# Seven products from the sixth chunk on, their weight sums formed earlier and brought by GpSimd's queue

## The chip, the cores and the metric

The kernel runs on one core of a Trainium2 chip. The metric is the device time of one execution in microseconds, median of several runs. The kernel before takes 916.63 us (three runs, 916.19 to 918.40).

## The reference, cut to what matters

Attention with pooled keys and values, and behind it a two-layer feed-forward network on the attention's output, all in fp32:

```
q, k, v: 8 batches x 8 heads x 576 x 64;   w_in: 512 x 2048;   w_out: 2048 x 512
k_p, v_p = mean of k, v over 8 neighbours       # 576 -> 72 keys
attn = softmax(q k_p^T / 8) ; o = attn v_p       # 8 x 8 x 576 x 64
x = o, heads side by side                        # 4608 tokens x 512
h = x @ w_in ; g = max(0.01 h, h) ; out = g @ w_out
```

## The kernel before, in words

The 4608 tokens are cut into nine chunks of 512 tokens, c0 to c8. The hidden 2048 columns are cut into 16 blocks of 128, f0 to f15, two of which form a "pair" later. TensorE has no fp32 product of full precision in this form, so each fp32 operand is held as a high part and the remainder (tiles xh and xl, gh and gl, pT_hi and pT_lo), and a product is three matmuls: high by high, low by high, high by low.

**Plain chunks.** For each f, the first layer takes 12 matmuls of 128x512 into one PSUM bank (`m1`, L1143 to L1145). ScalarE applies the leaky ReLU in place (L1148) and casts the high part gh (L1151), VectorE subtracts for gl (L1152). Two f's later the second layer takes 12 matmuls (`add_up`, L1354 to L1356) into four accumulators, one for each 128 tokens. At a chunk's end these are copied out and stored (`store`). So TensorE does 24 matmuls of 512 columns for one f, 48 for two.

**Seven-product chunks.** From chunk FAST on (before: c6, c7, c8), the first layer of a pair is one product of 2x2 blocks, done with seven products of half-size blocks instead of eight. Each is 6 matmuls of 128x256 (`product`, L1261), 42 for a pair, and the second layer's 24 matmuls follow (`pair`). The sums of blocks of x (T1 to T4) are made by `combine` (GpSimd L798, ScalarE L793, VectorE L794). The sums of blocks of w_in (S1 to S4, and the block A22 for the first four pairs) do not depend on x. They are formed once for each of the eight pairs, in the plain chunks, by `prepare`: nine VectorE additions of 128x256 (L1183), four ScalarE casts (L1186) and four VectorE subtractions (L1190), with the tile x_tail as scratch. High and low parts are put in "places", the unused second halves of the next chunk's x tiles, and from there stored to a DRAM tensor `kept` with eight transfers of 128 KB (L1217), and one of 256 KB for A22 (L1220). When the pair is multiplied, `stream` (L1253) brings the sums back, three loads for a pair: S1 with S2 (512 KB) into one "seat", S3 (256 KB) into a half of a w tile, S4 with A22 (512 or 256 KB) into another seat. The first pair's loads are issued by SyncE, the others by ScalarE's queue, each as soon as the product that reads the old contents is done; nothing is loaded for a chunk's last pair, since the next chunk runs the pairs in reverse.

**Attention beside it.** The attention of the next chunk's tokens runs in small steps ("units") that are dealt out between the matmuls of a chunk: scores (pss, L600), maximum (L608), exponential (L610), normalising on GpSimd (L644, L650; tile `at`), then a transposition through DRAM: SyncE stores rows (L661) and fetches blocks (L670), VectorE transposes them (L681, tile pp), ScalarE and VectorE split them (L703, L706, L710), and TensorE multiplies with v (pa, L725 to L728). The sums over 8 keys or values are made by GpSimd (L265, L272) from tiles that SyncE loads (L288, L305, L318).

**What sets the order.** TensorE's order is written out by hand throughout. In the plain chunks c0 to c5 the other engines' instructions are put in an order by the framework's scheduler from that. From the first seven-product chunk on GpSimd and SyncE are taken in the order of the program as well. `PLAN` says in which run of a chunk the weight sums are formed: (how many pairs, from which beat, until which). The runs are: c0 and c1 with f0 to f7 (run 0; runs 1 and 2, a half of c1 each), c1 with f8 to f15 (run 3), c0 with f8 to f15 (run 4, named REST), and then c2 to c8 whole.

Of the kernel before, what the change touches and what calls it, by code (L numbers as in the profile page):

```python
# [10 lines left out]
F32 = mybir.dt.float32  # L11
# [13 lines left out]
def tile_pooled_attention_ffn(  # L25
# [9 lines left out]
    nc = tc.nc  # L35
# [34 lines left out]
    VIA = 2  # L70
    SPLIT = 8
    HALF = CH // 2
    FAST = 6
    NEAR = (FAST + 1) % 2


# [1047 lines left out]
    REST = len(runs) - 1  # L1124
# [47 lines left out]
    def prepare(j, places):  # L1172

        f0, f1 = PAIRS[j]
        (a11, a12), (a21, a22) = (
            [[ws[0, f].bitcast(F32)[:, part, half] for part in range(2)]
             for half in (slice(0, HALF), slice(HALF, DM))] for f in (f0, f1)
        )
        u, w = (x_tail[:, 2 * i : 2 * i + 2, :].rearrange("p k x -> p (k x)") for i in range(2))
        ADD, SUB = ALU.add, ALU.subtract  # L1180

        def do(out, a, b, op):
            nc.vector.tensor_tensor(out, a, b, op=op)  # L1183

        def high(i, of):
            nc.scalar.copy(places[i][0], of)  # L1186

        def low(i, of):
            h, l = places[i]
            nc.vector.tensor_tensor(l, of, h.bitcast(F32), op=SUB)  # L1190

        do(u, a21[0], a21[1], ADD)
        do(w, u, a22[0], ADD)
        yield
        do(w, w, a22[1], ADD)
        high(1, w)
        do(u, a11[0], u, SUB)
        yield
        do(u, u, a11[1], ADD)
        high(0, u)  # L1200
        low(1, w)
        yield
        do(w, w, a11[0], SUB)
        low(0, u)
        yield
        do(w, w, a11[1], SUB)
        high(2, w)
        do(u, a12[0], w, SUB)
        yield
        do(u, u, a12[1], ADD)  # L1210
        high(3, u)
        low(2, w)
        yield
        low(3, u)
        for i, parts_of in enumerate(places):
            for k, part in enumerate(parts_of):
                nc.sync.dma_start(kept[j, :, i, k, :], part.bitcast(F32))  # L1217
        if j < OPEN:
            with tc.issue_after(sent[-1].ins):
                nc.sync.dma_start(kept[j, :, 4], ws[0, f1].bitcast(F32)[:, :, HALF:])  # L1220
        yield

    def free(n, i):

        if n < REST + FAST - 2:
            return [(h[:, HALF:], l[:, HALF:]) for h, l in zip(*x_parts(runs[n][0] + 1))]
        side, part = (runs[n][0] + 2) % 2, "hl"[i % 2]
        x = [one.tile([P, CH], F32R, tag=f"x{part}{side}_{kk}", name=f"place{i}_{kk}") for kk in range(NK)]
        return [(y[:, :HALF], y[:, HALF:]) for y in x]
# [36 lines left out]
    def pair(n, c, j, then, old, hooks):  # L1266


        f0, f1 = PAIRS[j]
        x = sums[c]  # L1270
        a11, a12 = ws[0, f0][:, :, :HALF], ws[0, f0][:, :, HALF:]
        a22 = seat("A22") if j < OPEN else ws[0, f1][:, :, HALF:]
        nm = f"{n}_{j}"
        pa, pc = ends_x[:, :HALF], ends_x[:, HALF:]
        pd, pe = ends_y[:, :HALF], ends_y[:, HALF:]
        off = one.tile([P, CH], F32, tag=f"xh{1 - NEAR}_{NK - 1}", name=f"off{nm}")
        dia = one.tile([P, CH], F32, tag=f"xl{1 - NEAR}_{NK - 1}", name=f"dia{nm}")

        def after(k):
            if hooks:  # L1280
                hooks[k]()

        def some(m):
            for _ in range(min(m, len(old))):
                old.pop(0)()
                yield

        def halves(w):
            h = three.tile([P, CH], F32R, tag="gh", name=f"gh{nm}")
            l = three.tile([P, CH], F32R, tag="gl", name=f"gl{nm}")  # L1290
            nc.scalar.copy(h, w)
            nc.vector.tensor_tensor(l, w, h.bitcast(F32), op=ALU.subtract)
            return h, l

        def load(name, ins):
            if then is not None:
                with tc.issue_after(ins.ins):
                    stream(nc.scalar, then, name)

        product(pa, a11, x["B11"], True)  # L1300
        product(pc, seat("S1"), x["T1"], False)
        with tc.high_priority():
            nc.scalar.copy(pd, pa)
            nc.scalar.copy(dia[:, HALF:], pc)
        yield
        yield from some(3)

        product(pd, seat("S2"), x["T2"], False)
        product(pa, a12, x["B21"], False)
        with tc.high_priority():  # L1310
            nc.vector.tensor_tensor(pe, pd, dia[:, HALF:], op=ALU.add)
            load("S1", nc.scalar.activation(dia[:, :HALF], pa, AF.Prelu, alpha=0.01))
        after(0)
        yield
        yield from some(2)

        product(pd, seat("S3"), x["T3"], False)
        with tc.high_priority():
            nc.vector.tensor_tensor(dia[:, HALF:], pd, dia[:, HALF:], op=ALU.add)
            load("S3", nc.scalar.activation(dia[:, HALF:], dia[:, HALF:], AF.Prelu, alpha=0.01))  # L1320
            gd = halves(dia)
        after(1)
        yield
        yield from some(len(old))

        product(pe, seat("S4"), x["B22"], False)
        product(pd, a22, x["T4"], False)
        with tc.high_priority():
            load("S4", nc.scalar.activation(off, ends_y, AF.Prelu, alpha=0.01))
            go = halves(off)  # L1330
        after(2)
        yield

        for f, t, g, i in (
            (f0, 0, gd, 0), (f0, 1, gd, 1), (f1, 2, gd, 2), (f1, 3, gd, 3),
            (f1, 0, go, 0), (f1, 1, go, 1), (f0, 2, go, 2), (f0, 3, go, 3),
        ):
            old.append(lambda f=f, t=t, g=g, i=i: second(n, c, f, t, g, i))
# [142 lines left out]
    for n, pieces in enumerate(beside):  # L1481
        us = [att[b][u] for b, u in line_up([x for x in pieces if x[0] < VIA])]
        us += [
            att[x[0]][x[1]] if x else lambda: None
            for x in line_of(n, [x for x in pieces if x[0] >= VIA])
        ]
        if n == 0:

            cut = us.index(att[1]["au01"]) + 1
            us, rest = us[:cut], us[cut:]  # L1490

            us.remove(att[1]["sa20"])
            us.insert(us.index(att[1]["au00"]) + 1, att[1]["sa20"])
            us = [att[0][u] for u in TAIL_STEPS.split()] + us
        elif n == 1:
            us = rest
        if n == REST:

            units[-1] = [lambda: None] * AHEAD + us[:AHEAD]
            us = us[AHEAD:]  # L1500
        units.append(us)
# [8 lines left out]
    for b, n in loads_at.items():  # L1510
        early[max(n, REST) - 1].append(b)

    PLAN = {REST + 1: (2, 10, 36), REST + 2: (3, 3, 34), REST + 3: (1, 3, 20), REST + 4: (2, 3, 34)}
    STEPS_OF = 7
    left = list(range(len(PAIRS)))

# [5 lines left out]
    for n, (c, fs, ts) in enumerate(runs[: REST + FAST - 1]):  # L1522
        us = list(units[n])
# [137 lines left out]
```

## Time and profile before

| | |
|---|---|
| median of the runs | 916.63 us (916.19 to 918.40) |
| the profiled execution | 919.39 us; span from first to last instruction 917.6 us |
| mean granted TensorE clock | 0.991 |
| busy: TensorE, VectorE, ScalarE, GpSimd | 886.1, 515.8, 447.4, 223.6 us |
| stages in the span | c0 and c1 until 212 us; run 4 212 to 264; c2 264 to 361; c3 361 to 457; c4 457 to 553; c5 553 to 640; c6 640 to 736; c7 736 to 824; c8 from 824 |

The stages are told apart by the program's names in the timeline of TensorE. The span is 1.8 us shorter than the time of the same execution. A row of the timeline gives the start of an instruction and its length; matmuls overlap, so the pace is read from one start to the next, not from the length.

### The profile page before, as it was taken

Reading aid. Unit: us, or ns where it says so; the run is one execution under the profiler, and the core shown is the slowest. Engines: PE = TensorE matmul, PEld = TensorE weight load, DVE = VectorE, ACT = ScalarE, POOL = GpSimd, SP = SyncE. Lnnn points to the kernel's source line nnn. Section 1 sums busy time; section 2 is a strip of 40 time slices with the busy share of each in tenths; the row PEclk is TensorE's granted clock in tenths of the full one; section 3 lists DMA queues with packets and bytes.
Section 4 is the critical chain, followed back from the end, with each engine's and each line's share of the span. In section 5 each row is a group of like instructions: output and inputs, shape, how many; then the busy total and the mean of one; then the engine's idle time right before and its main releaser. Section 6 shows DMA issues by size and latency. Waiting matters only on the chain.

```text
span 917.6 us, 14146 instructions
## 1 busy us (share of the span) xinstructions
PE 886.1 (97%) x4731; PEld 764.1 (83%) x4731; DVE 515.8 (56%) x1229; ACT 447.4 (49%) x1397; POOL 223.6 (24%) x394
## 2 busy tenths in 40 slices
PE   5599999999999999999999999999999999999998
PEld 4478888788887888888888888888999999999997
DVE  6999569546276654774465537655665653342222
ACT  5788559345344534443454336354654553453322
POOL 4511110352534231412133132514320230010000
PEclk9889999999999999999999999999999999999999
DMA  9965231327357342834245317630785255425332
GB/s 266 313 203 171 64 76 47 88 61 197 102 163 169 109 96 53 230 93 109 53 141 118 97 36 195 162 102 3 198 212 148 67 148 144 122 78 161 104 113 72
DMA packets 157464, 116.53 MB, mean 127 GB/s; under 512 B 100688, under 2 KB 136016, under 8 KB 157392
## 3 DMA queue, kind: packets, MB, share of 16 engines
q1 hardware_dynamic: 145488, 90.86, 36.7%
q10 hardware_dynamic: 11904, 24.78, 9.4%
q8 instruction: 37, 0.61, 0.3%
q14 instruction: 35, 0.29, 0.1%
HBM read 85.07 MB, written 30.54 MB: 126 GB/s over the span
## 4 chain that ended last, share of the span: by engine, by line
PE 84%; DVE 7%; ACT 3%; DMA 2%; POOL 1%; issue 1%; SPq 1%; POOLq 0%; DVEq 0%; ACTq 0%
PE acc L1354 13%; PE acc L1355 13%; PE acc L1356 13%; PE ph L1143 8%; PE ph L1144 8%; PE ph L1145 8%; PE ends_y L1261 7%; PE ends_x L1261 6%; PE pss L600 3%; DMA kremraw<-in_k_dram 1%; PE pa L726 1%; DMA blocks<-rows 1%; PE pa L728 1%; PE pa L727 1%; PE pa L725 1%
## 5 line engine op out<-in xcount | busy, mean ns | idle before, releaser
L1354 PE MATMUL acc<-w,gh 128*128 128x512 f32 x576 | 228.2, 396 | 0.7 <-DVE o L1394 0.7
L1355 PE MATMUL acc<-w,gh 128*128 128x512 f32 x576 | 225.9, 392 | 0.0
L1356 PE MATMUL acc<-w,gl 128*128 128x512 f32 x576 | 225.0, 391 | 0.0
L1143 PE MATMUL ph<-xh,w 128*128 128x512 f32 (+1 forms) x416 | 159.5, 384 | 0.6 <-DVE gl L1152 0.6
L1144 PE MATMUL ph<-xl,w 128*128 128x512 f32 (+1 forms) x416 | 156.5, 376 | 0.0
L1145 PE MATMUL ph<-xh,w 128*128 128x512 f32 (+1 forms) x416 | 156.3, 376 | 0.0
L1356 PEld LDWEIGHTS acc<-w,gl 128*128 128x128 f32 x576 | 108.4, 188 | 23.5
L1354 PEld LDWEIGHTS acc<-w,gh 128*128 128x128 f32 x576 | 108.7, 189 | 20.1 <-issue 1.1
L1355 PEld LDWEIGHTS acc<-w,gh 128*128 128x128 f32 x576 | 108.7, 189 | 18.1
L610 ACT ACTIVATE e<-pss,red 128x72 f32<-128x72 f32 (+1 forms) x320 | 97.8, 329 | 44.6 <-DVE red L608 44.5
L1148 ACT ACTIVATE ph<-ph 128x512 f32<-128x512 f32 (+1 forms) x104 | 57.7, 555 | 94.8 <-PE ph L1145 94.3
L1152 DVE TENSOR_TENSOR gl<-ph,gh 128x512 fp32r<-128x512 f32 (+1 forms) x104 | 66.8, 642 | 61.3 <-ACT gh L1151 60.8
L644 POOL TENSOR_TENSOR at<-e,red 128x128 f32<-128x128 f32 (+1 forms) x120 | 50.1, 438 | 173.9 <-DVE red L641 90.9
L1143 PEld LDWEIGHTS ph<-xh,w 128*128 128x128 f32 x416 | 79.2, 190 | 14.6 <-DVE gl L1152 1.2
L1145 PEld LDWEIGHTS ph<-xh,w 128*128 128x128 f32 x416 | 79.0, 190 | 14.3
L1144 PEld LDWEIGHTS ph<-xl,w 128*128 128x128 f32 x416 | 79.1, 190 | 13.1
L610 ACT ACTIVATION_READ_ACCUMULATOR e<-pss,red 128x1 f32 (+1 forms) x320 | 68.6, 214 | 0.0
L681 DVE STREAM_TRANSPOSE pp<-blocks 128x384 f32<-128x384 f32 (+1 forms) x60 | 44.2, 758 | 41.2 <-DMA blocks<-rows 41.2
L608 DVE TENSOR_REDUCE red<-pss 128x4 f32<-128x288 f32 (+1 forms) x80 | 35.8, 453 | 52.9 <-PE pss L600 51.5
L703 ACT CAST pT_hi<-pp 128x384 fp32r<-128x384 f32 (+1 forms) x80 | 36.8, 479 | 52.5 <-DVE pp L681 48.7
L1151 ACT CAST gh<-ph 128x512 fp32r<-128x512 f32 (+1 forms) x104 | 57.8, 556 | 2.6
L600 PEld LDWEIGHTS pss<-kT,qT 128*128 128x128 f32 x320 | 45.8, 195 | 8.4 <-ACT qT L577 2.2
(290 smaller groups left out, 1486.2 us busy)
## 6 DMA issues: line engine op xcount, KB each, us to landing
seat<-kept ACTq DMA_DIRECT2D x31, 512.0 KB
rows<-at SPq DMA_DIRECT2D x48, 192.0 KB
blocks<-rows SPq DMA_DIRECT2D x48, 192.0 KB
out_dram<-o SPq DMA_DIRECT2D x34, 256.0 KB
w_bits<-in_moe_w_in_dram SPq DMA_DIRECT2D x16, 512.0 KB
w_bits<-in_moe_w_out_dram SPq DMA_DIRECT2D x16, 512.0 KB
q<-in_q_dram SPq DMA_DIRECT2D x96, 64.0 KB
w<-kept ACTq DMA_DIRECT2D x21, 256.0 KB
```

What stands on the lines that cost most here:

```text
L600: nc.tensor.matmul(sc[:, 2 * SP * i : 2 * SP * (i + 1)], qT[:, p, :], kT[:, p, :, :].rearrange("d i s -> d (i s)"), start=True, stop=True,)
L610: ins = nc.scalar.activation(e[:n, h, :], scv[:n, h, :], AF.Exp, bias=mx[:n, h : h + 1], accum_out=sm[:n, h : h + 1],)
L1143: nc.tensor.matmul(ph, w[:, 0, ks], xh[kk][:, r], start=kk == 0, stop=False)
L1144: nc.tensor.matmul(ph, w[:, 0, ks], xl[kk][:, r], start=False, stop=False)
L1145: nc.tensor.matmul(ph, w[:, 1, ks], xh[kk][:, r], start=False, stop=kk == NK - 1)
L1148: nc.scalar.activation(ph, ph, AF.Prelu, alpha=0.01)
L1151: casts.append(nc.scalar.copy(gh, ph))
L1152: lows.append(nc.vector.tensor_tensor(gl, ph, gh.bitcast(F32), op=ALU.subtract))
L1261: nc.tensor.matmul(out, w[:, stay, ks], move, start=start and i + n == 0, stop=i + n == 3, skip_group_check=True,)
L1354: nc.tensor.matmul(a, gh[:, r], hi, start=first, stop=False)
L1355: nc.tensor.matmul(a, gh[:, r], lo, start=False, stop=False)
L1356: nc.tensor.matmul(a, gl[:, r], hi, start=False, stop=last)
```

## The change

`FAST` is 5 instead of 6: c5 is a seven-product chunk as well. The sums of the weights must then be complete a chunk earlier. `PLAN` starts in run 4: two pairs there, one in c2, three in c3, two in c4 (before: two in c2, three in c3, one in c4, two in c5). The places in run 4 are the second halves of c2's x tiles. The eight stores of a pair to `kept` are issued one by one behind each low part, instead of together at the pair's end. The loads from `kept` for all pairs but the first are issued from GpSimd's queue instead of ScalarE's. One empty step is put into the attention units of the run REST, so that what follows in that list comes half a step later.

```diff
-    FAST = 6
+    FAST = 5
     NEAR = (FAST + 1) % 2
...
         def low(i, of):
             h, l = places[i]
             nc.vector.tensor_tensor(l, of, h.bitcast(F32), op=SUB)
+            for k, part in enumerate(places[i]):
+                nc.sync.dma_start(kept[j, :, i, k, :], part.bitcast(F32))
...
         low(3, u)
-        for i, parts_of in enumerate(places):
-            for k, part in enumerate(parts_of):
-                nc.sync.dma_start(kept[j, :, i, k, :], part.bitcast(F32))
         if j < OPEN:
             with tc.issue_after(sent[-1].ins):
                 nc.sync.dma_start(kept[j, :, 4], ws[0, f1].bitcast(F32)[:, :, HALF:])
...
         if n < REST + FAST - 2:
-            return [(h[:, HALF:], l[:, HALF:]) for h, l in zip(*x_parts(runs[n][0] + 1))]
+            return [(h[:, HALF:], l[:, HALF:]) for h, l in zip(*x_parts(n - REST + 2))]
...
             if then is not None:
                 with tc.issue_after(ins.ins):
-                    stream(nc.scalar, then, name)
+                    stream(nc.gpsimd, then, name)
...
         if n == REST:
 
+            us.insert(2, lambda: None)
             units[-1] = [lambda: None] * AHEAD + us[:AHEAD]
             us = us[AHEAD:]
...
-    PLAN = {REST + 1: (2, 10, 36), REST + 2: (3, 3, 34), REST + 3: (1, 3, 20), REST + 4: (2, 3, 34)}
+    PLAN = {REST: (2, 1, 14), REST + 1: (1, 3, 17), REST + 2: (3, 5, 36), REST + 3: (2, 3, 34)}
```

**SyncE's queue in c2.** The rows are the transfers around the fetch of the blocks of tiles 3 and 4 (blocks_3_0, blocks_4_0), which the first pa of c2 waits for. Names: kremraw and v0raw are loads of the next batch's keys and values, rows and blocks the transposition's two halves, q the next queries. Before:

```order
L661 DMA rows_4_1_3019<-at_4_1_3015 64x4x96
L1217 DMA kept<-xl_0_2961 128x256
L305 DMA kremraw_3278<-in_k_dram 64x1x512
L288 DMA v0raw_3302<-in_v_dram 64x2x512 x2
L670 DMA blocks_3_0_3123<-rows_3_0_2870 128x384
L670 DMA blocks_4_0_3157<-rows_4_0_2981 128x192
L661 DMA rows_0_0_3111<-at_0_0_3107 128x4x96
L461 DMA q_4_3370<-in_q_dram 32x16x32 x3
```

In the changed kernel the same place reads so:

```order
L1192 DMA kept<-xl_2_2904 128x256
L661 DMA rows_4_1_3085<-at_4_1_3081 64x4x96
L1192 DMA kept<-xh_3_2901 128x256
L1192 DMA kept<-xl_3_2905 128x256
L305 DMA kremraw_3320<-in_k_dram 64x1x512
L288 DMA v0raw_3341<-in_v_dram 64x2x512
L670 DMA blocks_3_0_3185<-rows_3_0_2932 128x384
L670 DMA blocks_4_0_3209<-rows_4_0_3045 128x192
L288 DMA v0raw_3341<-in_v_dram 64x2x512
L661 DMA rows_0_0_3176<-at_0_0_3172 128x4x96
```

The two fetches stand behind one load of v0raw instead of two; the whole of the pair's `kept` stores stands ahead of them.

**VectorE in c2, from the transposition of those blocks to the split that pa needs.** pp is the transposed tile, pT_lo and pT_hi its two parts, gl the low part of a hidden block, L1183 and L1190 belong to the weight sums. Before:

```order
L1152 TENSOR_TENSOR gl_4_3080<-ph_4_3045,gh_4_3079 128x512
L1183 TENSOR_TENSOR x_tail<-x_tail,w_4_657 128x256
L681 STREAM_TRANSPOSE pp_3_0_3125<-blocks_3_0_3123 128x4x96
L681 STREAM_TRANSPOSE pp_4_0_3159<-blocks_4_0_3157 128x2x3x32
L1183 TENSOR_TENSOR x_tail<-w_4_657,x_tail 128x256
L1190 TENSOR_TENSOR xl_2_2963<-x_tail,xh_2_2959 128x256
L706 TENSOR_TENSOR pT_lo<-pp_3_0_3125,pT_hi 128x2x128
L1183 TENSOR_TENSOR x_tail<-x_tail,w_4_657 128x256
L710 SCALAR_TENSOR_TENSOR pT_hi<-pp_3_0_3125,marks,pT_hi 128x128
L706 TENSOR_TENSOR pT_lo<-pp_4_0_3159,pT_hi 128x2x64
L710 SCALAR_TENSOR_TENSOR pT_hi<-pp_4_0_3159,marks,pT_hi 128x64
```

In the changed kernel:

```order
L681 STREAM_TRANSPOSE pp_3_0_3187<-blocks_3_0_3185 128x4x96
L1152 TENSOR_TENSOR gl_4_3148<-ph_4_3113,gh_4_3147 128x512
L681 STREAM_TRANSPOSE pp_4_0_3211<-blocks_4_0_3209 128x2x3x32
L706 TENSOR_TENSOR pT_lo<-pp_3_0_3187,pT_hi 128x2x128
L710 SCALAR_TENSOR_TENSOR pT_hi<-pp_3_0_3187,marks,pT_hi 128x128
L706 TENSOR_TENSOR pT_lo<-pp_4_0_3211,pT_hi 128x2x64
L710 SCALAR_TENSOR_TENSOR pT_hi<-pp_4_0_3211,marks,pT_hi 128x64
```

The three operations on weight sums between the transposition and the split are gone from here; gl_4 has come between the two transpositions.

**GpSimd in the first seven-product chunk.** Before, that is c6: GpSimd has no transfers, and after the carried tokens' copies its row is the normalising of one tile after another (at), a fill with zeros, and at the end the combining:

```order
L644 TENSOR_TENSOR at_2_0_6739<-e_2_0_6687,red_2_0_6688 128x4x32 x2
L650 TENSOR_TENSOR at_2_0_6739<-e_2_0_6687,red_2_0_6688 128x4x32
L644 TENSOR_TENSOR at_2_1_6765<-e_2_1_6697,red_2_1_6698 128x4x32 x2
L650 TENSOR_TENSOR at_2_1_6765<-e_2_1_6697,red_2_1_6698 128x4x32
L555 MEMSET qT_4_6844 128x4x64
L644 TENSOR_TENSOR at_3_0_6855<-e_3_0_6779,red_3_0_6780 128x4x32 x2
```

In the changed kernel, for the pairs in the middle of c5 (seat and w_9 are the loads from `kept`, k0raw and k1raw belong to the sums of the last batch's keys):

```order
L1252 DMA seat_5721<-kept 128x1024
L1252 DMA w_9_1193<-kept 128x2x256
L265 TENSOR_TENSOR k0raw_6182<-k0raw_6182 128x2x256
L265 TENSOR_TENSOR k0raw_6182<-k0raw_6182 128x2x128
L272 TENSOR_TENSOR ksum_6179<-k0raw_6182 128x128
L644 TENSOR_TENSOR at_1_0_6320<-e_1_0_6257,red_1_0_6258 128x4x32 x2
L650 TENSOR_TENSOR at_1_0_6320<-e_1_0_6257,red_1_0_6258 128x4x32
L1252 DMA seat_5724<-kept 128x512
L265 TENSOR_TENSOR k1raw_6185<-k1raw_6185 128x2x256
L265 TENSOR_TENSOR k1raw_6185<-k1raw_6185 128x2x128
L272 TENSOR_TENSOR ksum_6179<-k1raw_6185 128x128
L644 TENSOR_TENSOR at_1_1_6386<-e_1_1_6267,red_1_1_6268 128x4x32 x2
```

GpSimd works its rows off in this order: a load that must wait until TensorE has read the old contents holds up the normalising (L644) behind it, and sums of keys that wait for their own load hold up the loads from `kept` behind them. In c5 there are 21 such loads, 84 in the whole kernel.

## Rows read from the trace of the kernel before

**Rows 1.** The page: busy time by engine, and the chain that ended last by engine.
```profile
PE 886.1 (97%) x4731; PEld 764.1 (83%) x4731; DVE 515.8 (56%) x1229; ACT 447.4 (49%) x1397; POOL 223.6 (24%) x394
...
PE 84%; DVE 7%; ACT 3%; DMA 2%; POOL 1%; issue 1%; SPq 1%; POOLq 0%; DVEq 0%; ACTq 0%
```
**Rows 2.** Windows by stage: start:end, length, busy PE PEld DVE ACT POOL, clock, DMA.
```profile
212.00:264.00 52.00, 52.00 (x249) 43.81 (x248) 24.39 (x53) 18.72 (x53) 18.63 (x29) 1.00 0.54 147
264.00:361.00 97.00, 94.86 (x443) 79.56 (x442) 57.10 (x140) 41.17 (x143) 31.29 (x51) 0.98 0.45 112
553.00:640.00 87.00, 86.79 (x410) 72.78 (x409) 53.95 (x131) 42.05 (x133) 29.05 (x50) 1.00 0.44 121
640.00:736.00 96.00, 96.00 (x620) 87.68 (x619) 57.69 (x139) 52.24 (x183) 20.63 (x39) 1.00 0.56 149
736.00:824.00 88.00, 88.00 (x557) 79.94 (x557) 36.12 (x75) 39.74 (x109) 12.74 (x21) 1.00 0.44 128
```
**Rows 3.** Waits of TensorE from 212 to 640 us: total, times, longest.
```profile
PE pa L726 <- DVE pT_lo L706: 2.1, 1, 2.1
PE acc L1354 <- DVE o L1394: 0.7, 1, 0.7
PE ph L1143 <- DVE gl L1152: 0.2, 1, 0.2
```
**Rows 4.** Timeline of TensorE, one f of a plain chunk (c5).
```profile
579.55 0.39 PE L1143 MATMUL ph<-xh,w 128*128 128x512 f32 x1
579.78 0.39 PE L1144 MATMUL ph<-xl,w 128*128 128x512 f32 x1
...
584.99 0.39 PE L1143 MATMUL ph<-xh,w 128*128 128x512 f32 x1
```
**Rows 5.** Timeline of TensorE, one pair of a seven-product chunk (c8).
```profile
865.67 0.28 PE L1261 MATMUL ends_x<-B118xh,w 128*128 128x256 f32 x1
865.79 0.28 PE L1261 MATMUL ends_x<-B118xl,w 128*128 128x256 f32 x1
...
876.21 0.28 PE L1261 MATMUL ends_x<-B118xh,w 128*128 128x256 f32 x1
...
876.93 0.28 PE L1261 MATMUL ends_x<-T18xh,seat 128*128 128x256 f32 x1
```
**Rows 6.** Timeline of TensorE around its longest wait behind 212 us (c2).
```profile
289.87 0.28 PE L725 MATMUL pa<-pT_hi,v_hi 128*128 128x256 f32 x1
292.29 0.39 PE L726 MATMUL pa<-pT_lo,v_hi 128*128 128x256 f32 x1 [2.14 <-DVE pT_lo L706]
...
293.54 0.63 PE L1355 MATMUL acc<-w,gh 128*128 128x512 f32 x1
...
296.53 0.51 PE L1145 MATMUL ph<-xh,w 128*128 128x512 f32 x1
```
**Rows 7.** Windows just behind it.
```profile
293.50:296.50 3.00, 3.00 (x8) 2.34 (x7) 2.34 (x7) 0.89 (x2) 0.00 (x0) 0.50 0.72 179
```
**Rows 8.** Timeline of VectorE at that place.
```profile
287.76 1.07 DVE L681 STREAM_TRANSPOSE pp<-blocks 128x384 f32<-128x384 f32 x2 [3.68 <-DMA blocks<-rows]
288.75 0.38 DVE L1183 TENSOR_TENSOR x_tail<-w,x_tail 128x256 f32<-128x256 f32 x1
289.05 1.38 DVE L1190 TENSOR_TENSOR xl<-x_tail,xh 128x256 fp32r<-128x256 f32 x1
290.35 0.61 DVE L706 TENSOR_TENSOR pT_lo<-pp,pT_hi 128x256 fp32r<-128x256 f32 x1
...
291.84 0.40 DVE L706 TENSOR_TENSOR pT_lo<-pp,pT_hi 128x128 fp32r<-128x128 f32 x1
```
**Rows 9.** The chain of waits there: start, length, what.
```profile
282.55 0.60 SPq L288
283.20 4.47 DMA blocks<-rows
```
**Rows 10.** Timeline of TensorE: a shorter wait at the start of c3.
```profile
368.00 0.40 PE L1356 MATMUL acc<-w,gl 128*128 128x512 f32 x1
369.05 0.47 PE L1354 MATMUL acc<-w,gh 128*128 128x512 f32 x1 [0.66 <-DVE o L1394]
369.36 0.40 PE L1355 MATMUL acc<-w,gh 128*128 128x512 f32 x1
```
**Rows 11.** Groups by line of VectorE: the weight sums (count, busy us, mean ns).
```profile
L1183 DVE TENSOR_TENSOR x_tail<-x_tail,w 128x256 f32<-128x256 f32 x48 | 21.2, 441 | 0.7 <-POOL x L775 0.4
...
L1190 DVE TENSOR_TENSOR xl<-x_tail,xh 128x256 fp32r<-128x256 f32 x24 | 12.8, 532 | 0.5 <-ACT xh L1186 0.5
```
**Rows 12.** Timeline of ScalarE's queue: a load of S1 with S2 (c8).
```profile
870.81 0.33 ACTq L1253 DMA_DIRECT2D seat<-kept  x1
```
**Rows 13.** Timeline of SyncE's queue in run 4: a 512 KB load, and the partial sums.
```profile
220.31 1.24 SPq L288 DMA_DIRECT2D k1raw<-in_k_dram  x2
...
244.55 6.38 SPq L1365 DMA_DIRECT2D partial<-partial  x2
```
**Rows 14.** Timeline of GpSimd: the first use of that load.
```profile
228.30 1.29 POOL L265 TENSOR_TENSOR k1raw<-k1raw 128x512 f32<-128x512 f32 x1 [1.25 <-DMA k1raw<-in_k_dram]
```

## The prediction

> **What bounds the kernel now.** I read the page's busy times and chain first. TensorE is busy 97% of the span, and 84% of the chain that ended last is TensorE [rows 1]. The windows by stage then say where the rest is: behind 212 us TensorE is idle only in c2 (94.86 of 97 us, clock 0.98) and for fractions in c3 and c5; in c6 and c7 it is busy throughout at full clock [rows 2]. So two things can move the time: fewer TensorE cycles, and a wait of TensorE that goes or comes. The list of TensorE's waits from 212 to 640 us has three rows, and one is large: pa on pT_lo, 2.1 us, in c2 [rows 3]. Everything ahead of 212 us stays as it is: the change begins in run 4.
>
> The profiled execution took 919.39 us, 2.76 us above the median 916.63. I sum on the profiled execution and take 2.76 off at the end. A difference of 0.3% (2.75 us) is about what a measurement of this kernel can tell from no change.
>
> **Part 1: c5 with seven products.** Plain chunk: from the first matmul of an f to that of the next 579.55 to 584.99, 5.44 us for 24 matmuls, 0.2267 each [rows 4]; two f's 10.88 us. Seven products: one pair 865.67 to 876.21, 10.54 us [rows 5]. Both stretches are free of attention, and the attention's matmuls are the same in either form, so the difference holds beside them: 0.34 us for a pair, eight pairs, **-2.7 us**. It is less than an eighth of the first layer because a matmul of 256 columns starts every 0.12 us [rows 5], not 0.113, and the second layer is unchanged. TensorE's own count can't be hidden: it is the bound.
>
> **Part 2: the wait in c2.** L725 starts at 289.87 and L726 only at 292.29, where a matmul of that size starts 0.12 us after the last: 2.3 us lost [rows 5, 6]. Behind it the granted clock is 0.50 from 293.5 to 296.5, its lower level of 1.2 GHz [rows 7]; seven intervals from 293.54 to 296.53 take 0.427 each instead of 0.227, 1.4 us more [rows 4, 6]. The wait costs 3.7 us in all. Its history: the fetch of the blocks was issued at 283.20, just behind the second half of v0raw, and took 4.47 us [rows 9]; VectorE idled 3.68 us for it, transposed at 287.76, and then did two operations on weight sums (288.75, and one of 1.38 us) ahead of the split, which began at 290.35; the second pT_lo, which pa needs, began at 291.84 [rows 8]. From landing to the end of that, 4.5 us.
>
> In the order of the changed kernel the weight sums are gone from this stretch of VectorE, and half of v0raw (256 KB) stands behind the blocks. Taking out 1.6 us of weight sums ahead of the split (288.75 to 290.35) and some 0.45 us of the one within it, and adding gl_4 (0.6 us), leaves about 3.0 us from landing. The 0.7 us of one v0raw issue (0.60 in rows 9) bring the fetch to 282.5, and with 256 KB less ahead of it, it lands by 286 to 287. Ready then at 289 to 290, against a need at 289.87. Bounds for this part: the wait goes whole, -3.7; it stays whole because the blocks come no earlier, 0 (and were both halves of the queue to land later, up to +1). I take **-3.7**, nearer to the first, since the 1.6 us of VectorE are certain and a remainder under 0.8 us costs no clock: the wait of 0.66 us in c3 was followed by matmuls at full pace (369.05, 369.36) [rows 10].
>
> **Part 3: weight sums in run 4.** What is formed is the same in number, eight pairs; it moves. A pair is nine additions of 0.44 and four subtractions of 0.53 us on VectorE, 6.1 us [rows 11]. Two pairs more in run 4 raise VectorE there from 24.4 to 36.6 us of 52, 0.70 of the stage; c2 has 0.59 and c5 0.62 [rows 2], and c5 shows a single wait of 0.2 us on VectorE [rows 3]. On SyncE's queue 16 stores of 128 KB and two of 256 KB stand among the loads of run 4. k1raw (issued at 220.31, first used at 228.30, 8 us for 512 KB) [rows 13, 14] now stands behind five to seven of these stores; v1raw, vremraw and the fetch of the partial sums (244.55) [rows 13] follow it. The partial sums land at about 251 and are needed when c0's accumulators are done, near 260: some 5 us of room, against 7 stores at about 0.4 to 0.6 us of issue each, 3 to 4 us. Bounds: 0, and a wait like the one in c2, +3.7. I take **+0.8**, by the small waits [rows 3, 10].
>
> **Part 4: loads from GpSimd's queue.** No row shows a transfer issued there, so I bound it. Before, S1 with S2 is issued at 870.81 [rows 12] and its first reader starts at 876.93 [rows 5]: landing within 6.1 us is free, and in c6 and c7, 14 such loads, TensorE is busy throughout [rows 2]. From below: an earlier issue cannot help TensorE, 0. From above: 8 us, as the 512 KB of k1raw needed in a crowded stretch [rows 13, 14], would be 1.9 us late in each of 28 pairs, +53 us. I take **0**: the seats' rows are long and contiguous, the DMA share in c6 and c7 is 0.44 to 0.56 [rows 2], and 512 KB needed less than 6.1 us there from the other queue; only an issue cost over some 2 us would be seen. The Trainium skill ("DMA: Bandwidth & Descriptors", section "Anatomy of one DMA — SWDGE (gpsimd) path") fits a transfer from GpSimd as 2.0 us and its bytes at 436 GB/s, which would be 3.2 us here, an estimate by that page; by it the sum is as I have it.
>
> **Part 5: GpSimd's order in c5.** It now holds the loads, the normalising and the sums of the last batch's keys and values in one fixed row. A load waits for TensorE to have read its seat, and the normalising behind it waits along, a pair's share of up to 5 or 7 us. Its result goes through two transfers and is needed 10 us or more later, so I put **+0.4** for one small wait [rows 3], with 0 and +3.7 as ends. GpSimd itself has room: 20.6 of 96 us in c6 [rows 2].
>
> The sum: 919.39 - 2.7 - 3.7 + 0.8 + 0.4 = 914.2; less 2.76 for the median, **911.4 us**, 0.57% faster.
>
> **Rivals.**
> A, slower: the loads from GpSimd come late. Place: S1's first product of each pair. Price: what they exceed 6.1 us by, times 28. It undoes the gain of 5.2 us at 0.19 us for each pair, a landing of 6.3 us; at 8 us the time is 965. For it: nothing of GpSimd's issue is in the trace, and in c5 the loads of v0raw, v1raw and vremraw stand in front of seat loads, so one late load of values delays a seat. Against it: the margin. The Trainium skill ("SBUF — State Buffer", box in section "SBUF: two separate sides") says that GpSimd cannot write descriptors for its transfers while VectorE runs a copy in its two-port mode; by that rule a seat load could be held for a VectorE instruction. The longest single VectorE instruction in the rows takes 1.38 us [rows 8], and held up once by that, the page's 3.2 us would still be inside the margin; no run here shows it. Chance 0.13.
> B, the wait in c2 only moves: the blocks land no earlier, or run 4 takes it over. Then 916.63 - 2.7 + 0 to 1 = 914 to 915. For it: the whole store of a pair stands ahead of the blocks now, and the next late thing in c2 is the second pair of blocks. Chance 0.20.
> C, crowding: the partial sums in run 4, or attention in c5, cost a wait with a fall of the clock, 3.7 us each. With one, 911.4 + 3.7 = 915.1; with two, 918.8. For it: queues that grow. Against it: slack of 5 us and more at either place. Chance 0.13.
> The forecast, both gains with waits under 2 us, 909 to 913.5: 0.54.
>
> **How the numbers follow.** Faster than 913.9: all of the forecast, half of B, a little of C, 0.66. Within 914 to 919.4: the rest of B, most of C, 0.19. Slower: A and the tail of C, 0.15. The range: down to 908.8 (916.63 less 6.4, and 1.4 for the waits of c3 and c5 that might go too), up to 918.
>
> **What would show it.** In the trace of the changed kernel: L1261 from about 550 us on, with pairs of 10.54 us without attention; no wait on pT_lo L706 in c2 and a granted clock of 1.00 there; no wait of TensorE on a seat; VectorE near 37 us in run 4. I am wrong if TensorE waits for seats (A), if c2's window keeps a clock of 0.98 (B), or if new waits over 2 us stand in run 4 or in c5 (C).

## The result, and the profile after

The changed kernel takes 924.96 us (median of six runs, 924.15 to 927.01), the kernel before 917.54 in the same runs: the ratio is 1.0077, with an interval of 1.0063 to 1.0091. It is 7.4 us slower. The forecast was 911.4 us, 5.2 us faster than the 916.63 known then, and its range ended at 918.

The page of the profiled execution (924.82 us): busy time by engine, and the chain by engine.

```profile
PE 888.2 (96%) x4875; PEld 769.4 (83%) x4875; DVE 537.2 (58%) x1244; ACT 458.5 (50%) x1428; POOL 283.1 (31%) x482
...
PE 70%; DVE 10%; DMA 7%; ACT 5%; POOL 3%; issue 2%; SPq 2%; DVEq 0%; POOLq 0%; ACTq 0%
```

Against [rows 1] TensorE's share of the chain has fallen from 84% to 70%; VectorE (7% to 10%) and transfers (2% to 7%) have taken most of the difference. The windows by stage answer to [rows 2] (run 4, c2, c5, c6, c7; the borders have moved by a few us):

```profile
214.00:266.00 52.00, 50.52 (x236) 40.91 (x235) 30.77 (x71) 21.83 (x60) 18.84 (x31) 1.00 0.61 178
266.00:363.00 97.00, 94.44 (x440) 79.10 (x439) 53.17 (x124) 39.55 (x137) 29.91 (x52) 0.98 0.43 104
550.00:643.00 93.00, 90.40 (x571) 81.19 (x570) 59.80 (x135) 49.38 (x177) 48.15 (x78) 1.00 0.68 184
643.00:738.00 95.00, 93.77 (x602) 85.28 (x601) 57.03 (x133) 50.59 (x169) 32.67 (x58) 1.00 0.56 150
738.00:826.00 88.00, 87.52 (x556) 79.37 (x555) 37.51 (x76) 39.82 (x108) 27.28 (x44) 1.00 0.43 125
```

TensorE now idles in every one of these stages: 1.5 us in run 4, 2.6 in c2, 2.6 in c5, 1.2 in c6, 0.5 in c7. The waits of TensorE name what it waits for (212 to 640 us against [rows 3], then from 640 us on, where before had none):

```profile
PE ph L1143 <- DVE gl L1152: 3.7, 2, 2.6
PE pss L600 <- DVE kT L489: 1.4, 1, 1.4
PE acc L1353 <- DVE o L1393: 1.2, 2, 0.8
PE acc L1355 <- DVE gl L1291: 0.8, 1, 0.8
PE pa L726 <- DVE pT_lo L706: 0.2, 1, 0.2
PE pa L728 <- DVE pT_hi L710: 0.2, 1, 0.2
...
PE ends_y L1260 <- DVE ends_y L1310: 1.2, 1, 1.2
PE ends_y L1260 <- DVE dia L1318: 0.5, 1, 0.5
```

Every releaser is VectorE; no row names a seat. The large wait on pT_lo is gone, and a larger one on gl stands in its place.

Where the time goes is best read by following one matmul through the kernels. The table has the start of L725, the first matmul of a pa, in each profiled execution, as a lag on the kernel before (its own starts: 230.89 in run 4, 309.45 in c2, 440.09 in c3, 807.60 in c7). "E" numbers are the experiments below.

| kernel | run 4 | c2 | c3 | c7 |
|---|---|---|---|---|
| changed kernel | 1.8 | 2.6 | 3.1 | 5.7 |
| E2 c5 plain, plan as changed | 2.5 | 3.8 | 4.5 | 4.5 |
| E8 one pair in run 4 | 2.6 | 0.0 | 0.2 | 4.8 |
| E9 one pair in run 4, later | 1.8 | -0.7 | 0.1 | 4.8 |
| E10 c5 plain, plan of before | 1.3 | -0.9 | -0.8 | 0.1 |
| E11 none in run 4 | 0.2 | -2.6 | -2.0 | 3.9 |
| E13 none in run 4, four in c3 | -0.2 | -3.0 | -3.1 | -1.4 |

Ahead of the change, at 128 us, these lags are -0.3 to 1.0, so a row is good to about 1 us. The lag from c3 to c7 holds c5's saving: 2.7 us less of matmuls, if Part 1 is right, against whatever waits come. The changed kernel loses 2.6 there, so its waits from c4 to c7 would cost 5.3 us. The saving can also be counted. Between those two L725, each form of matmul times its median step from one start to the next adds up to 365.65 us before and 362.38 in the changed kernel (an estimate from these two traces): 3.3 us less. The stretch takes 1.9 us more than that before and 7.8 in the changed kernel, so the waits cost 5.3 to 5.9 us. Set against the forecast, the steps are: run 4, forecast +0.8, measured +2.1 (from 128 us); c2, -3.7 and +0.8; c3, 0 and +0.5; c4 to c7, -2.3 and +2.6.

The executions with a lag near -2 in c2 show that the 3.7 us in the profile of the kernel before [rows 6, 7] are dear even for that kernel. E5 differs from it only by the loads of c6 to c8, and there the same pa waited 1.5 us and no fall of the clock followed (its lag in c2 is -2.5).

### The profile page after: what moved, and what is told of

Same layout as the page of the kernel before. It is cut to its first block, busy times and chain, and to the rows that moved or that the text cites. A ratio compares the mean times of both kernels' runs of the same rounds, so it can differ in the third digit from the quotient of the medians.

```text
span 923.0 us, 14554 instructions
## 1 busy us (share of the span) xinstructions
PE 888.2 (96%) x4875; PEld 769.4 (83%) x4875; DVE 537.2 (58%) x1244; ACT 458.5 (50%) x1428; POOL 283.1 (31%) x482
## 4 chain that ended last, share of the span: by engine, by line
PE 70%; DVE 10%; DMA 7%; ACT 5%; POOL 3%; issue 2%; SPq 2%; DVEq 0%; POOLq 0%; ACTq 0%
PE acc L1353 11%; PE acc L1354 11%; PE acc L1355 11%; PE ends_y L1260 9%; PE ends_x L1260 6%; PE ph L1143 5%; PE ph L1145 5%; PE ph L1144 5%; PE pss L600 3%; DVE x_tail L1183 1%; DMA kremraw<-in_k_dram 1%; ACT e L610 1%; DMA blocks<-rows 1%; DMA out_dram<-o 1%; SPq L318 1%
## 5 line engine op out<-in xcount | busy, mean ns | idle before, releaser
L1143 PE MATMUL ph<-xh,w 128*128 128x512 f32 (+1 forms) x352 | 134.8, 383 | 4.6 <-DVE gl L1152 4.5
L1145 PE MATMUL ph<-xh,w 128*128 128x512 f32 (+1 forms) x352 | 131.8, 374 | 0.0
L1144 PE MATMUL ph<-xl,w 128*128 128x512 f32 (+1 forms) x352 | 131.7, 374 | 0.0
L1148 ACT ACTIVATE ph<-ph 128x512 f32<-128x512 f32 (+1 forms) x88 | 48.5, 551 | 72.8 <-PE ph L1145 72.7
L1143 PEld LDWEIGHTS ph<-xh,w 128*128 128x128 f32 x352 | 67.0, 190 | 17.4 <-DVE gl L1152 6.6
L1152 DVE TENSOR_TENSOR gl<-ph,gh 128x512 fp32r<-128x512 f32 (+1 forms) x88 | 55.9, 635 | 43.7 <-ACT gh L1151 43.3
L1252 POOL DMA_DIRECT2D seat<-kept x56 | 31.5, 563 | 160.9 <-PE ends_y L1260 153.4
L644 POOL TENSOR_TENSOR at<-e,red 128x128 f32<-128x128 f32 (+1 forms) x120 | 49.0, 430 | 99.8 <-DVE red L641 73.5
L1145 PEld LDWEIGHTS ph<-xh,w 128*128 128x128 f32 x352 | 66.9, 190 | 11.8
L1144 PEld LDWEIGHTS ph<-xl,w 128*128 128x128 f32 x352 | 67.0, 190 | 10.6
```

Source lines behind the costliest of these rows:

```text
L644: nc.gpsimd.tensor_tensor(at[:n, :, i, :].rearrange("a (h f) j -> a h f j", h=2), e[:n, 2 * i : 2 * i + 2, 0:MAIN].rearrange("a h (f j) -> ...
L1143: nc.tensor.matmul(ph, w[:, 0, ks], xh[kk][:, r], start=kk == 0, stop=False)
L1144: nc.tensor.matmul(ph, w[:, 0, ks], xl[kk][:, r], start=False, stop=False)
L1145: nc.tensor.matmul(ph, w[:, 1, ks], xh[kk][:, r], start=False, stop=kk == NK - 1)
L1148: nc.scalar.activation(ph, ph, AF.Prelu, alpha=0.01)
L1152: lows.append(nc.vector.tensor_tensor(gl, ph, gh.bitcast(F32), op=ALU.subtract))
```

## The experiments

Times are medians; the kernel before, run beside them, took 917.6 to 917.9 us in each set. Ratios are to it, with their intervals.

**E1. ScalarE's queue again.**

```diff
-                    stream(nc.gpsimd, then, name)
+                    stream(nc.scalar, then, name)
```

> The changed kernel with one part undone: the loads of the weight sums are issued from ScalarE's queue again, as before. Theory 1 (transfers: in c5 the loads meet the last batch's queries, keys and values, and the queries come late whoever issues): waits of TensorE in c5 to c7 stay near 5.8 us, time 924 to 926. Theory 2 (GpSimd's fixed row: loads that wait for TensorE hold up the normalising, and this the rows, blocks and queries on SyncE): most of these 5.8 us go, time 919 to 921.

Measured: 930.01 us (1.0128; 1.0115 to 1.0141), 5 us slower than the changed kernel. Neither theory's time came: GpSimd's queue keeps the change from being worse. ScalarE's timeline in c5 of this run:

```profile
603.14 0.42 ACT L1319 ACTIVATE dia<-dia 128x256 f32<-128x256 f32 x1 [1.52 <-DVE dia L1318]
605.13 0.39 ACTq L1252 DMA_DIRECT2D w<-kept  x1
605.56 0.62 ACT L1290 CAST gh<-dia 128x512 fp32r<-128x512 f32 x1 [2.00 <-DMA rows<-at]
606.18 0.60 ACT L1328 ACTIVATE off<-ends_y 128x512 f32<-128x512 f32 x1
608.92 0.33 ACTq L1252 DMA_DIRECT2D seat<-kept  x1
609.29 0.62 ACT L1290 CAST gh<-off 128x512 fp32r<-128x512 f32 x1 [2.52 <-DMA v0raw<-in_v_dram]
609.82 0.35 ACT L703 CAST pT_hi<-pp 128x192 fp32r<-128x192 f32 x1
```

The two loads are issued 1.6 and 2.1 us after the instruction ahead of them on ScalarE ended (603.56 to 605.13, 606.78 to 608.92), and the cast behind each stands that long; the split pT_hi is thrown back too, and TensorE waits for it:

```profile
610.22 0.41 PE L725 MATMUL pa<-pT_hi,v_hi 128*128 128x320 f32 x1 [4.07 <-ACT pT_hi L703]
```

**E2. c5 plain, all else as changed.**

```diff
-    FAST = 5
+    FAST = 6
```

> The changed kernel with c5 as a plain chunk again (FAST 6); weight sums from run 4 on, early stores, GpSimd's queue and the empty step stay. If c5's seven products cost more by their waits than they save (3.8 us in c5 and 2.0 in c6 and c7 against 2.7 saved): 921 to 923, with the waits of run 4, c2 and c3 (2.9, 4.8 and 1.3 us) unchanged. Rival (the loss is in forming the sums early, and c5 itself pays): about 927.

Measured: 925.18 us (1.0081; 1.0068 to 1.0094), 0.2 us from the changed kernel. So in this plan c5's seven products bring nothing net, and the 7 us are lost with c5 plain as well. Neither expectation's number came; the time is between the two. The lag is complete by c3 (4.5 us in the table).

**E3. Stores at the pair's end.** Attention writes tokens into two of the places before the stores of run 4 here, so a part of one pair's sums is kept wrong; the instructions are the same in number.

```diff
-            for k, part in enumerate(places[i]):
-                nc.sync.dma_start(kept[j, :, i, k, :], part.bitcast(F32))
...
         low(3, u)
+        for i, parts_of in enumerate(places):
+            for k, part in enumerate(parts_of):
+                nc.sync.dma_start(kept[j, :, i, k, :], part.bitcast(F32))
```

> The changed kernel with one part undone: the eight stores of a pair are issued together at the pair's end. Theory 3 (each early store waits on SyncE's queue for its low part, and the loads of the next keys and the blocks stand behind it): the wait of TensorE in c2 on gl (2.7 us and 1.4 us at the lower clock) goes, time 920 to 922. Rival (SyncE's queue is not what holds the blocks): 924 to 926 with the wait in c2 still there.

Measured: 923.45 us (1.0060; 1.0048 to 1.0072), 1.5 us faster than the changed kernel. In c2 TensorE waits 1.8 us instead of 2.7 and the clock stays up, but in c3 it waits 2.0 with a fall of the clock behind it. The intervals of the two kernels overlap, so the 1.5 us are not clear of the spread. Nor is theory 3 tested in c2: the fetch of the blocks is issued at 285.31 (285.30 in the changed kernel), still behind two stores, and TensorE waits less because it comes there later (lag 2.8 instead of 1.8 in run 4). Whatever the stores cost, issuing them together does not bring the 7 us back.

**E4. No empty step.**

```diff
-            us.insert(2, lambda: None)
```

> The changed kernel without the empty step in the attention units of run 4. If the half step of delay is what brings the blocks of tiles 3 and 4 late in c2 (fetch issued at 285.30 against 283.20 before), the 4.1 us there go: 920 to 922. If the empty step is neutral or protects the start of c2: 924 to 928.

Measured: 927.15 us (1.0107; 1.0085 to 1.0128), slower by 2.2 us on the medians, the intervals just overlapping. In the profiled execution the step protects the start of run 4: without it pa waits there for both halves of the split (1.3 us on pT_hi, 2.2 on pT_lo; 0.2 in the changed kernel), and the lag is 5.6 there instead of 1.8.

**E5 and E6. GpSimd's queue alone, and the empty step alone, in the kernel before.**

```diff
-                    stream(nc.scalar, then, name)
+                    stream(nc.gpsimd, then, name)
```

> The kernel before with the loads from kept issued from GpSimd's queue, and nothing else. With ScalarE's queue the changed kernel took 5 us more, because ScalarE's casts stood behind loads that were issued late in c5. Before, c6 to c8 have 0.3 us of waits, so there is nothing to win: 917 to 918.5. Rival (GpSimd's fixed row delays the normalising in c6): 919 to 921.

```diff
+            us.insert(2, lambda: None)
```

> The kernel before with the empty step in run 4's attention, and nothing else. The changed kernel lost 2.2 us without it, at the start of run 4, where pa waited for pT_lo. Before, run 4 has no wait, so it can only move the wait of c2: by half a step the need at 289.87 and the fetch move alike; 917 to 919. Rival (the delay gives c2's blocks their time): the 3.7 us go, 914 to 915.

Measured: 918.68 us (1.0011; 0.9999 to 1.0023) and 918.59 us (1.0007; 0.9997 to 1.0016). Neither costs or gains anything that can be told.

**E7. An eighth of the bytes in c5.**

```diff
+        if small and name == "S3":
+            to, of = to[:, :1, : HALF // 4], of[:, :1, : HALF // 4]
+        elif small:
+            to, of = to[:, :1, :1, : HALF * m // 4], of[:, :1, :1, : HALF * m // 4]
```

> The changed kernel, but in c5 each load from kept brings only an eighth of its bytes (64 KB for S1 with S2, 32 KB for S3, and so on), so c5's sums are mostly those of an earlier pair; the number of loads, their order and their waits stay. Theory 1 (the bytes of the loads meet the last batch's queries, keys and values in c5, so that queries, blocks and stores come late): the DMA share in c5 falls from 0.8 to about 0.6 and TensorE's 3.8 us of waits in c5 go to under 1.5; time 921.5 to 923. Rival (VectorE's own work and fixed order hold TensorE up, not the transfers): the waits stay, 924 to 926.

Measured: 924.31 us (1.0075; 1.0062 to 1.0087). Windows from 540 to 640 us, here and then in the changed kernel:

```profile
540.00:640.00 100.00, 98.59 (x615) 88.49 (x614) 60.79 (x137) 52.16 (x183) 44.98 (x79) 1.00 0.41 98
```

```profile
540.00:640.00 100.00, 97.40 (x608) 87.31 (x607) 61.40 (x136) 51.54 (x181) 46.70 (x78) 1.00 0.62 169
```

The DMA share falls by a third and TensorE's idle time from 2.6 to 1.4 us, but the median does not fall clear of its spread: the stages ahead of c5 scatter by as much (the lag in c3 is 4.2 here and 3.1 in the changed kernel). E14 repeats it on a calmer kernel.

**E8. One pair in run 4, two in c2. E9. The same, begun seven beats later.**

```diff
-    PLAN = {REST: (2, 1, 14), REST + 1: (1, 3, 17), REST + 2: (3, 5, 36), REST + 3: (2, 3, 34)}
+    PLAN = {REST: (1, 1, 14), REST + 1: (2, 3, 34), REST + 2: (3, 5, 36), REST + 3: (2, 3, 34)}   # E8
+    PLAN = {REST: (1, 8, 16), REST + 1: (2, 3, 34), REST + 2: (3, 5, 36), REST + 3: (2, 3, 34)}   # E9
```

> The changed kernel with one pair of weight sums formed in run 4 instead of two, and two in c2 instead of one. If the density of VectorE's work at the start of run 4 makes its small waits (2.9 us from 205 to 222 us against none before): they fall to about 1, time 922 to 923.5. Rival (it only moves them into c2): 925 or more, with longer waits in c2.

> The changed kernel with one pair in run 4 as in the run with one pair (923.9), but begun seven beats later, behind the copies of c1's accumulators; two pairs in c2. If the place in VectorE's order matters and not the amount: the lag at the first pa of run 4 falls from 2.4 to under 0.7 and the time to 921.5 to 922.5. Rival (any sums in run 4 cost the same): 923.5 to 924.5.

Measured: 923.89 us (1.0065; 1.0051 to 1.0078) and 922.09 us (1.0039; 1.0025 to 1.0052). One pair fewer leaves the loss in run 4 where it was (from 128 us to the table's pa 2.4 us, 2.1 in the changed kernel). Beginning later, when half of the copies of c1's accumulators are done, brings that to 1.1, more than the 0.7 expected, and the wait on those copies is gone from the list. So in run 4 the place in VectorE's order counts for more than the amount. The 1.8 us between the two medians are less certain: the intervals touch, and the two profiled executions end alike (lag 4.8 in c7). Waits of TensorE from 200 to 235 us, E8 and then E9:

```profile
PE pa L726 <- DVE pT_lo L706: 1.3, 1, 1.3
PE acc L1353 <- DVE o L1393: 0.9, 1, 0.9
PE ph L1143 <- DVE gl L1152: 0.7, 1, 0.7
```

```profile
PE ph L1143 <- DVE gl L1152: 1.1, 1, 1.1
PE pa L726 <- DVE pT_lo L706: 0.4, 1, 0.4
```

**E10. c5 plain and the plan of before.** The other three edits stay.

```diff
-    FAST = 5
+    FAST = 6
...
+    PLAN = {REST + 1: (2, 10, 36), REST + 2: (3, 3, 34), REST + 3: (1, 3, 20), REST + 4: (2, 3, 34)}
```

> The changed kernel with c5 plain (FAST 6) and the plan of before (nothing formed in run 4, two pairs in c5); early stores, GpSimd's queue and the empty step stay. Against the run with FAST 6 and the new plan (925.2) this changes the plan alone. If forming earlier is the loss of some 7 us: 917.5 to 919.5. Rival (the early stores or the three small edits together carry it): 922 or more.

Measured: 918.68 us (1.0009; 1.0000 to 1.0017). It differs from E2 by the plan alone, and is 6.5 us faster. With c5 plain, the plan carries the loss.

**E11. None in run 4, three pairs in c4. E12. The same with an eighth of c5's bytes.**

```diff
+    PLAN = {REST + 1: (2, 10, 36), REST + 2: (3, 5, 36), REST + 3: (3, 3, 34)}
```

> The changed kernel with no weight sums in run 4: two pairs in c2, three in c3, three in c4; c5 still has seven products. If forming in run 4 is what costs there (TensorE falls 2.1 us back at its start, where the copies of c1's accumulators wait on VectorE behind the sums, and again in c2): the lag on the kernel before at the pa of run 4 falls from 2.1 to about 0.4, and at the end of c3 from 3.4 to under 0.5; c5 to c7 still cost 2.6 net, time 919.5 to 921. Rival (c4 with three pairs makes up for it with waits of its own): 923 to 925.

> No weight sums in run 4, and in c5 each load from kept brings an eighth of its bytes (so c5's sums are mostly those of an earlier pair). Both suspected costs taken away: if they add, 2.1 us less than without sums in run 4 alone, 917 to 919. Rival (VectorE's order in c5 to c7 is what costs, whatever the transfers): within 0.7 us of the run without sums in run 4.

Measured: 924.04 us (1.0076; 1.0055 to 1.0096) and 924.99 us (1.0077; 1.0063 to 1.0092). Run 4 and c2 are mended (0.2 and -2.6 in the table), and c4 takes the gain back. Timeline of TensorE in c4 of E11:

```profile
493.11 0.39 PE L1145 MATMUL ph<-xh,w 128*128 128x512 f32 x1
494.30 0.42 PE L725 MATMUL pa<-pT_hi,v_hi 128*128 128x320 f32 x1 [0.80 <-ACT pT_hi L703]
496.71 0.42 PE L726 MATMUL pa<-pT_lo,v_hi 128*128 128x320 f32 x1 [1.99 <-DVE pT_lo L706]
```

The rival's wait came, in a chunk that had none, with the lower clock behind it (0.57 from 498 to 502 us). The lead on the changed kernel falls from 5.2 us in c3 (L725 at 438.06 against 443.21) to 0.3 at the end of c4 (531.71 against 532.01). E12 has the same wait, and its median is no lower.

**E13. None in run 4, four pairs in c3, two in c4. E14. The same with an eighth of c5's bytes.**

```diff
+    PLAN = {REST + 1: (2, 10, 36), REST + 2: (4, 3, 50), REST + 3: (2, 3, 34)}
```

> The changed kernel with nothing formed in run 4: two pairs in c2, four in c3 (until beat 50 of 64), two in c4. Without sums in run 4 the kernel was 5.2 us ahead of the changed one at the end of c3, and lost 4.6 us again in c4, where three pairs held up a split that pa waited for. If the crowding of c4 by the third pair is that loss: no wait over 1 us in c4, time 919 to 920.5. Rival (a fourth pair in c3 makes the same wait there): 923 to 925 with a wait over 2 us in c3.

> The same with an eighth of the bytes in c5's loads from kept (so c5's sums are mostly those of an earlier pair). If the transfers are what c5 to c7 lose most by: 1.5 to 2.5 us less than the run with four pairs in c3. Rival (VectorE's fixed order holds TensorE up there, whatever the transfers): within 0.8 us of it, and the waits on VectorE rows L1310, L1318 and L489 stay.

Measured: 919.43 us (1.0013; 1.0001 to 1.0026) and 917.56 us (0.9997; 0.9987 to 1.0007). With seven products in c5 and only the plan altered, 5.5 of the 7.4 us are back. Even so c5's saving does not show: E10, with c5 plain, is 0.75 us faster than E13, and their intervals overlap. E14 is 1.9 us faster than E13 on the medians, with overlapping intervals as well. The profiled spans differ by 0.8 (915.9 and 915.1), but E14 has that lead before c5 begins (lag in c3 -3.9 against -3.1), and from c3 to c7 both lose 1.7 us. The same stretch costs 2.1 us less with an eighth of the bytes in E7 than in the changed kernel, and 1.0 less in E12 than in E11. So what the bytes cost is not settled. What remains in E14 are waits on VectorE, most of them in the seven-product chunks, as the rival had it (200 to 915 us; L1322 and L1314 are L1318 and L1310 of the changed kernel):

```profile
PE ends_y L1264 <- DVE dia L1322: 1.7, 3, 1.0
PE ends_y L1264 <- DVE ends_y L1314: 1.2, 2, 0.7
PE pa L726 <- DVE pT_lo L706: 0.9, 1, 0.9
PE acc L1357 <- DVE o L1397: 0.8, 1, 0.8
```

No version tried beats the kernel before clear of the spread.

## Why the prediction was wrong, point by point

**Part 1, c5's products: right in size.** The count above gives 2.7 to 3.3 us between c3 and c7. E2 and the changed kernel differ by c5 alone and end 0.2 us apart, so as much is lost again in waits. That the saving is TensorE's own count held; that it could be spent again was left to part 5.

**Part 2, the wait in c2: the step that failed first.** The forecast had the split ready at 289 to 290 and the wait gone. But "adding gl_4 (0.6 us)" priced a hidden block's low part by its length alone. In the new order it stands behind the transposition that waits for the blocks, and TensorE waits for gl_4 eighteen matmuls before it comes to that pa. In the kernel before it comes to that place at 285.79, with gl_4 done at 283.75. The forecast's own landing of 286 to 287 would already have made gl_4 late. TensorE before, then VectorE and TensorE in c2 of the changed kernel:

```profile
285.79 0.39 PE L1143 MATMUL ph<-xh,w 128*128 128x512 f32 x1
```

```profile
289.19 0.86 DVE L681 STREAM_TRANSPOSE pp<-blocks 128x384 f32<-128x384 f32 x1 [4.46 <-DMA blocks<-rows]
289.89 0.67 DVE L1152 TENSOR_TENSOR gl<-ph,gh 128x512 fp32r<-128x512 f32 x1
...
291.54 0.28 DVE L706 TENSOR_TENSOR pT_lo<-pp,pT_hi 128x128 fp32r<-128x128 f32 x1
291.75 2.05 DVE L710 SCALAR_TENSOR_TENSOR pT_hi<-pp,marks,pT_hi 128x64 fp32r<-128x64 f32 x1
```

```profile
287.67 0.39 PE L1355 MATMUL acc<-w,gl 128*128 128x512 f32 x1
290.62 0.50 PE L1143 MATMUL ph<-xh,w 128*128 128x512 f32 x1 [2.56 <-DVE gl L1152]
```

All profiled executions bear this out. In the eight kernels with sums in run 4 (the changed one, E1 to E4, E7 to E9) gl_4 stands behind the transposition, and TensorE's wait in c2 is on gl, 1.1 to 3.7 us in all. In the eight without (the one before, E5, E6, E10 to E14) gl_4 stands ahead of it, and the wait is on pT_lo, 0.9 to 2.1 us.

The blocks did not come earlier either. Their fetch was issued at 285.30, where 282.5 was forecast and 283.20 was the time before [rows 9]. SyncE's queue shows no gap ahead of it: the pair's stores, kremraw and the half of v0raw follow one another.

```profile
284.55 0.66 SPq L288 DMA_DIRECT2D v0raw<-in_v_dram  x1
285.30 1.02 SPq L670 DMA_DIRECT2D blocks<-rows  x2
```

The split itself was ready only in part. TensorE's need, moved by the lag of 1.8 us, is 291.65, and the second pT_lo starts at 291.54. But the last piece, L710, took 2.05 us instead of the 0.28 of the kernel before and ended at 293.80, and the last of pa's four matmuls reads it. So a wait of nearly 2 us may have been left even with gl_4 ahead of the transposition; no run moves gl_4 alone.

The chosen -3.7 was also the full price of one execution: 919.39 us is 1.8 above the median of all runs of before, and in E5 the same wait cost 1.5 us. The sum took the whole wait off and then 2.76 us for the median as well, so part of it seems to have been taken off twice.

**Part 3, sums in run 4: mis-sized.** Forecast +0.8, with +3.7 as the end. The changed kernel falls 2.1 us behind from 128 us to the second pa of run 4, and the plan as a whole costs 6.5 (E10 against E2). The density was worked out for all of run 4 (36.6 us of 52; measured 30.8), but the sums begin at its first beat, where VectorE also copies c1's accumulators and splits two tiles; from 205 to 223 us it is busy 14.2 of 18:

```profile
205.00:223.00 18.00, 16.20 (x72) 12.01 (x71) 14.20 (x38) 9.43 (x33) 2.92 (x8) 1.00 0.70 208
```

Against E8, E9 begins its one pair later, and the lag at that pa is 0.8 us less. The partial sums, which the forecast watched, are issued from 251.36 on instead of 244.55, and no wait of TensorE or VectorE is put down to them.

**Part 4, GpSimd's queue: no seat came late, and the queue was worth more than nothing.** The page of the changed kernel gives the landing that no row of before had (last figure, us from issue):

```profile
seat<-kept POOLq DMA_DIRECT2D x42, 512.0 KB, 3.8
...
w<-kept POOLq DMA_DIRECT2D x28, 256.0 KB, 3.2
```

3.8 us is well inside the 6.1, and rival A is out by this row: no wait of TensorE is on a seat. The Trainium skill's fit ("DMA: Bandwidth & Descriptors", section "Anatomy of one DMA — SWDGE (gpsimd) path") gives 3.2 us, an estimate by that page, 0.6 short. The Trainium skill also says, in the section "Issuing engines are not separate DMA queues" of that page, that issuing from several engines saves only the sequencer's time for it, which is usually small beside the transfer. Here it is not small: E1 differs by the issuing engine alone and takes 5 us more, with ScalarE's casts standing behind the loads.

**Part 5, GpSimd's order in c5: the wrong engine watched.** Forecast +0.4; the waits from c4 to c7 cost 5.3 to 5.9. No row shows TensorE waiting on the normalising; it waits on VectorE, in the order of VectorE's own row. In c5 a transposition of queries waits for its load, and gl and the keys' kT wait behind it (0.8 and 1.4 us of TensorE). VectorE in c5:

```profile
570.98 1.13 DVE L565 STREAM_TRANSPOSE qT<-q 128x512 f32<-128x512 f32 x1 [2.62 <-DMA q<-in_q_dram]
571.96 1.26 DVE L1291 TENSOR_TENSOR gl<-dia,gh 128x512 fp32r<-128x512 f32 x1
573.14 0.61 DVE L484 STREAM_TRANSPOSE kT<-ksum 32x128 f32<-32x128 f32 x2
```

In c6 the transpositions of queries and keys, from 662.63 to 664.56 without a pause, stand ahead of the sum L1310 that TensorE waits for (1.2 us). How much of all this is due to the bytes of c5's loads is open (0.1 to 2.1 us in three pairs of executions, E13 and E14 above). Which of the rest is the last batch's keys and values, and which the queries, was not tried.

**The rivals.** B came nearest (the wait in c2 moves, run 4 takes some over), but its 914 to 915 added at most 1 us for it. C had the mechanism, crowding, with a price of 3.7 at two places; it came at five (run 4, c2, c3, c5, c6), so its 918.8 was short. A time above 919.4 was given 0.15, to A and the tail of C.

## What to carry to other kernels

When a moved instruction lands behind one that waits, price it by who waits for it, not by its length: TensorE stood 2.7 us for a gl of 0.67 us, and the clock fell behind it. Work that is formed beside the bound needs a place, not only room on average: the same sums cost 6.5 us more in the plan of the change than in that of before, and mending one crowded place (E11) made another until the fourth pair found a quiet one (E13). And a wait seen in one profiled execution is worth only what it costs in the median one.

## What the runs showed of the hardware that was not expected

A load issued by ScalarE held ScalarE up 1.6 and 2.1 us in c5 of E1, though TensorE's last read of the first one's old contents was over at 602.64. The seat loads take 0.56 us on GpSimd in the changed kernel and landed in 3.8 (median). During the first of the two waits SyncE was at two fetches of blocks; during the second it stood idle for its last 1.0 us. So what holds the issue is not shown. SyncE in E1:

```profile
602.15 3.23 SPq L670 DMA_DIRECT2D blocks<-rows  x2
```

A wait of the same length is not always followed by the lower clock. After 2.7 us without a matmul at 287.67 the changed kernel shows a granted clock of 0.62 in the next 4 us; after 2.7 us in the same place E7 shows 1.00. The rows, of the changed kernel and of E7:

```profile
290.60:294.60 4.00, 3.98 (x11) 3.18 (x12) 3.85 (x7) 1.43 (x3) 3.84 (x6) 0.62 0.68 156
```

```profile
293.30:296.30 3.00, 2.83 (x12) 2.33 (x13) 3.00 (x6) 1.57 (x4) 3.00 (x6) 1.00 0.64 128
```

The twelve matmuls behind the wait take 4.4 us in the one (from 290.62) and 2.9 in the other (from 293.47). That is 1.5 us between two executions of the same code at that place, and part of the scatter of these kernels.

Some VectorE instructions took longer while GpSimd computed. In the changed kernel the gl of a seven-product chunk (L1291, from dia or off) takes at most 0.69 us in the 44 cases without a GpSimd computation beside it and up to 1.76 in the 20 with one. The gl of a plain chunk (L1152), whose ph lies in PSUM, never takes more than 0.69. The L710 of 2.05 us above ran beside GpSimd's sums of v0raw and ended 0.08 us behind the first of them:

```profile
292.44 2.08 POOL L265 TENSOR_TENSOR v0raw<-v0raw 128x512 f32<-128x512 f32 x2
```

```profile
740.15 1.76 DVE L1291 TENSOR_TENSOR gl<-dia,gh 128x512 fp32r<-128x512 f32 x1
```

With c5 as a seven-product chunk its gl comes from SBUF. The gl that TensorE waits for at 573.27 took 1.26 us, beside GpSimd's normalising.
